# End of the attention stage ordered by hand, with expert 0's first block and half of its second product ahead of the token counts

## The chip, the cores and the metric

One NeuronCore of a Trainium2 chip runs the whole program in one launch. Its engines work side by side, each through its own list of instructions: TensorE (PE, the matrix products), VectorE (DVE), ScalarE (ACT), GpSimd (POOL) and SyncE (SP, which here only issues DMAs). The metric is the device time of one launch in microseconds; lower is better. Before the change it is 1738.94 us (median of three runs, 1738.03 to 1742.51).

## The reference

```python
# attention: q, k, v are (4, 8, 576, 64); nine chunks of 64 tokens, each by itself
scores = q_c @ k_c.T / sqrt(64); scores -= scores.max(-1)
attn = exp(scores); attn /= attn.sum(-1) + 1e-9
x = (attn @ v_c)                     # as 2304 tokens of 512
# mixture of experts, top 1, 8 experts, capacity 2304 // 8 * 2 = 576 tokens each
logits = x @ w_gate; expert = argmax(logits); gate_w = softmax(logits)[expert]
for each expert e, for its first 576 tokens in order:
    y = relu(x @ w1[e]) @ w2[e]      # 512 -> 1024 -> 512
    out[token] = gate_w * y          # the others stay zero
# second mixture, dense: P = softmax(x @ w2_gate) made doubly stochastic in 8 rounds
out = sum over e of P[:, e] * (relu(x @ w21[e]) @ w22[e])
```

The products of the experts are done with each fp32 operand split into two fp16 numbers (hi and lo), hi*hi + hi*lo + lo*hi.

## The kernel before

**Attention.** The 2304 tokens are 18 tiles of 128 (NT = 18). A loop over n runs 14 steps per iteration, each on another tile: step `f` with lag `l` works on tile n - l, in the order of the table `order`. For one tile the steps are: `st_tr` transposes K and Q on TensorE, `st_scores` the score product, `st_max` (VectorE) subtracts the row maximum and leaves `d`, `st_dtr` transposes `d`, `st_exp` (ScalarE), `st_pv` the product with V, `st_x1` (VectorE) divides and leaves the tile's `x`, `st_norm`, `st_scale`, `st_hi` and `st_lo` split `x` into fp16 rows which a DMA writes to `xs_d` in DRAM, `st_xtr`, `st_xcopy` and `st_logits` make the gate's logits. Every engine takes its instructions in the order in which this Python code issues them; nothing is reordered later.

**Routing.** Every three tiles are a group g (NG = 6). `route(g)` finds each token's expert (`r_max` to `r_tot`), its position among that expert's tokens (`r_mm` on TensorE, `r_sel`, `r_pos`), builds a table of token numbers by expert and position (`r_ge` to `r_col`, then `r_tab` on TensorE and `r_acc`, which adds it to `tacc`, for the last group to `gidx`), and the token's gate weight (`r_gw` to `r_kx`, `r_out` with its DMA to `xs_d`). The pieces are dealt out between the attention steps.

**Expert 0 early.** When group 3 (`EG`) is in the table, the first 256 tokens of expert 0 are known. `early_gather` fetches their rows into the weight area `wall`, `turn_into` transposes them into `e_xT`, and `first_product` runs four groups of 24 matmuls (L353), each followed by `hidden` (relu and split into `e_hh`, `e_hl`). This goes on beside the routing of groups 4 and 5. A matmul with `gohx` (L821) then makes the counts per expert.

**Experts.** `blocks(x, ...)` does a block of 256 or 128 tokens of expert x: first product, relu, second product (`y`, L901, 24 matmuls of 512 columns per 128 tokens), then a square sum, a scale and two writes (`x2_d`, `rk_d`). Lists called `sites` are dealt out behind its parts: the weights of the next expert are loaded (`w_load`), squared and summed (`w_stat`, L168, on ScalarE), turned into a scale (`w_scale`, L177, a small TensorE matmul that needs all four `w_stat`; `w_scale2` on VectorE), and split into hi (ScalarE) and lo (VectorE, for two quarters GpSimd) by `w_split`. Expert 0 has 512 tokens or fewer here but more than 384: after its block of 256 come two of 128 by `further`, whose rows ("late") are gathered once `gidx` is there. The raw second weights of expert 0 and expert 1 share one buffer (`stb`): expert 1's are loaded after the last split of expert 0's.

## Time and profile before

| | |
|---|---|
| median of three runs | 1738.94 us |
| the profiled execution | 1738.75 us, its span 1736.7 us |
| PE busy | 1697.3 us, 98% of the span |
| DVE, ACT, POOL busy | 69%, 54%, 42% |
| granted PE clock, mean | 0.994 |
| PE share of the chain of waits | 70% |

The profile is of one execution. Span is the time from its first to its last instruction; the execution's own time is 2.05 us longer. Busy shares are over the whole span, so a stage of 50 us hardly shows in them: the stages have to be read by windows. A granted clock of 1.00 is TensorE's 2.4 GHz, 0.50 is 1.2 GHz. In a timeline row the bracket at the end is idle time of the engine ahead of the row, with what ended it.

### The profile page before, as it was taken

How to read it: one execution, taken by the hardware profiler on the slowest of the kernel's cores; microseconds unless marked ns; L12 is line 12 of the kernel's file. 1: busy time of each engine (PE TensorE's matmuls, PEld its weight loads, DVE VectorE, ACT ScalarE, POOL GpSimd, SP SyncE). 2: the span in 40 equal slices, each digit the busy share in tenths (PEclk: the TensorE clock that was granted, in tenths of full speed). 3: DMA queues.
4: the chain of work that ended last, by engine and by line, in shares of the span. 5: the costliest groups of instructions: out<-in, count | busy, mean ns of one | idle time of the engine just before them, and what ended most of it. 6: DMA issues, size and time to landing. Idle time of an engine off the chain costs nothing.

```text
span 1736.7 us, 33835 instructions
## 1 busy us (share of the span) xinstructions
PE 1697.3 (98%) x13419; PEld 1233.8 (71%) x13419; DVE 1192.7 (69%) x2329; ACT 946.5 (54%) x1794; POOL 721.8 (42%) x765
## 2 busy tenths in 40 slices
PE   8999999989999999999999999999999999999997
PEld 7875666655555677777777777777777767777776
DVE  6886856855577766777676767677866686677554
ACT  6866756764445664655455546455643655354431
POOL 2325644622022334552445435354534543453443
PEclk9989999999999999999999999999999999999999
DMA  9948957735252413242243233223323241323201
GB/s 219 246 157 242 250 159 187 204 112 149 80 185 64 155 54 123 70 171 98 80 150 113 85 111 137 107 86 113 136 84 134 65 176 53 125 68 124 92 35 49
DMA packets 140335, 219.09 MB, mean 126 GB/s; under 512 B 62304, under 2 KB 80832, under 8 KB 140160
## 3 DMA queue, kind: packets, MB, share of 16 engines
q1 hardware_dynamic: 134768, 199.46, 36.3%
q0 software_dynamic: 5392, 17.26, 3.6%
q8 instruction: 115, 1.88, 0.5%
q14 instruction: 60, 0.49, 0.1%
HBM read 167.56 MB, written 41.91 MB: 121 GB/s over the span
## 4 chain that ended last, share of the span: by engine, by line
PE 70%; DVE 5%; ACT 1%; issue 1%; POOL 1%; POOLq 0%; ACTq 0%; DVEq 0%
PE p_m L1349 36%; PE p_m L1445 28%; PE p_m L1493 5%; DVE wall L297 3%; DVE acc L1416 1%; ACT wall L296 1%; PE p_m L1237 0%; ACT eh L1354 0%; POOL out_dram L1427 0%; DVE el L1357 0%; ACT tq L1389 0%; POOL el L1361 0%; DVE tq L1364 0%; DVE tq L1367 0%; DVE wall L255 0%
## 5 line engine op out<-in xcount | busy, mean ns | idle before, releaser
L1349 PE MATMUL p_m<-x,wall 128*128 128x384 f16 x4032 | 666.2, 326 | 3.4 <-ACT tq L1389 2.9
L1445 PE MATMUL p_m<-wall,eh 128*128 128x256 f16 x3528 | 580.3, 273 | 0.0
L1361 POOL TENSOR_TENSOR el<-tq,eh 128x384 f16<-128x384 f32 x336 | 346.9, 1060 | 560.0 <-ACT eh L1354 559.2
L1349 PEld LDWEIGHTS <-wall 128*128 128x128 f16 x4032 | 394.0, 98 | 260.3 <-issue 5.5
L1445 PE MATMUL p_m<-wall,el 128*128 128x256 f16 x1764 | 480.8, 273 | 0.0
L1354 ACT ACTIVATE eh<-tq 128x384 f16<-128x384 f32 x540 | 274.1, 522 | 189.1 <-DVE tq L1367 101.4
L1445 PEld LDWEIGHTS <-eh 128*128 128x128 f16 x3528 | 344.3, 98 | 44.3
L1416 DVE SCALAR_TENSOR_TENSOR acc<-p_m,cf,acc 128x256 f32<-128x256 f32 (+1 forms) x378 | 175.6, 521 | 130.3 <-PE p_m L1445 130.3
L1364 DVE TENSOR_TENSOR tq<-p_m,tq 128x384 f32<-128x384 f32 x288 | 158.4, 556 | 126.3 <-PE p_m L1349 125.3
L1445 PEld LDWEIGHTS <-el 128*128 128x128 f16 x1764 | 172.6, 98 | 20.0
L1357 DVE SCALAR_TENSOR_TENSOR el<-tq,eh 128x384 f16<-128x384 f32 x204 | 175.1, 860 | 10.0 <-ACT eh L1354 8.6
L1367 DVE SCALAR_TENSOR_TENSOR tq<-tq 128x384 f32<-128x384 f32 x252 | 133.1, 553 | 2.9
L353 PEld LDWEIGHTS <-wall 128*128 128x128 f16 x1344 | 108.6, 99 | 19.4 <-issue 6.1
L1389 ACT COPY tq<-p_m 128x384 f32<-128x384 f32 x96 | 45.7, 476 | 111.3 <-PE p_m L1349 107.6
L1493 PE MATMUL p_m<-wall,eh 128*128 128x512 f16 x288 | 85.6, 379 | 0.0
L1402 ACT ACTIVATE tq<-tq 128x384 f32<-128x384 f32 x84 | 43.9, 522 | 70.7 <-DVE tq L1364 70.7
L275 POOL TENSOR_TENSOR tq<-stb 128x256 f32<-128x256 f32 x56 | 48.7, 870 | 80.6 <-DVE wsumsq L184 58.9
L296 ACT ACTIVATE wall<-stb,wsb 128x256 f16<-128x256 f32 (+1 forms) x56 | 31.3, 605 | 92.0 <-DMA wb_d<-wall 66.6
L353 PE MATMUL p_p<-xT,wall 128*128 128x256 f16 x672 | 75.6, 272 | 4.8 <-PEq L1125 2.1
L275 POOL TENSOR_TENSOR tq<-sta 128x256 f32<-128x256 f32 x56 | 43.5, 776 | 82.5 <-DVE wall L297 48.7
L247 POOL TENSOR_SCALAR stb<-stb,wsb 128x1024 f32<-128x1024 f32 x16 | 54.6, 3415 | 53.6 <-DVE tq L1364 44.9
L297 DVE SCALAR_TENSOR_TENSOR wall<-stb,wsb,wall 128x256 f16<-128x256 f32 (+1 forms) x56 | 38.6, 703 | 47.1 <-ACT wall L296 44.8
(283 smaller groups left out, 2113.8 us busy)
## 6 DMA issues: line engine op xcount, KB each, us to landing
x<-xt_d SPq DMA_DIRECT2D x147, 384.0 KB, 3.6
wb_d<-wall SPq DMA_DIRECT2D x20, 896.0 KB, 3.5
wall<-wb_d SPq DMA_DIRECT2D x20, 896.0 KB, 6.4
sta<-in_moe_w_dram SPq DMA_DIRECT2D x32, 512.0 KB, 7.8
stb<-in_moe_w_dram SPq DMA_DIRECT2D x32, 512.0 KB, 6.8
sta<-in_moe_w_dram SPq DMA_DIRECT2D x16, 1024.0 KB, 6.3
stb<-in_moe_w_dram SPq DMA_DIRECT2D x16, 1024.0 KB, 7.8
xt_d<-x SPq DMA_DIRECT2D x21, 384.0 KB, 4.1
```

Of the source, the lines that this page charges most:

```text
L275: nc.gpsimd.tensor_tensor(out=at(o), in0=at(u), in1=at(v), op=op)
L297: nc.vector.scalar_tensor_tensor(out=o[:, cs, 1], in0=src, scalar=m.s, in1=o[:, cs, 0], op0=ALU.mult, op1=ALU.subtract)
L353: nc.tensor.matmul(p[:, f4, :], lhsT=w[:, kk, f * 128:(f + 1) * 128], rhs=xT[:, lo + kk, 0:W], start=(n == 0), stop=(n == 3 * KD - 1))
L1349: nc.tensor.matmul(p, lhsT=wt[:, w, lw, kk, :], rhs=xt[:, lx, kk, :], start=first and n == 0, stop=n == 5, skip_group_check=not first)
L1354: nc.scalar.activation(out=hs[op][0][:, q, :], in_=src, func=AF.Relu if op in (A11, A12, A22) or plain else AF.Copy)
L1357: nc.vector.scalar_tensor_tensor(out=hs[op][1][:, q, :], in0=src, scalar=0.0, in1=hs[op][0][:, q, :], op0=ALU.max, op1=ALU.subtract)
L1361: nc.gpsimd.tensor_tensor(out=hs[op][1][:, q, :], in0=src, in1=hs[op][0][:, q, :], op=ALU.subtract)
L1364: nc.vector.tensor_tensor(out=o, in0=a, in1=b, op=ALU.add)
L1367: nc.vector.scalar_tensor_tensor(out=o, in0=a, scalar=0.0, in1=b, op0=ALU.max, op1=op)
L1416: nc.vector.scalar_tensor_tensor(out=acc[:, j, cols], in0=y, scalar=coefs[x][:, j:j + 1], in1=acc[:, j, cols], op0=ALU.mult, op1=ALU.add)
L1445: nc.tensor.matmul(bk.t[:, cols], lhsT=hs[op][lh][:, q, t * 128:(t + 1) * 128], rhs=b.q[q][:, w, lw, :], start=m in (1, 5) and q == 0 and ...
L1493: nc.tensor.matmul(y.t, lhsT=h[:, kk % 4, c * 128:(c + 1) * 128], rhs=w[:, kk, :], start=(n == 0), stop=(n == 3 * KF - 1))
```

## The change

What it does:

- The loop over tiles ends at n = 18; what came in five more iterations is written out as one list of calls.
- K is transposed by a step of its own (`st_ktr`) at the head of an iteration; the steps `st_xtr` and `st_xcopy` move behind `st_pv`, and the routing pieces are dealt out behind `st_max` (but in iteration 18 over all steps).
- Gate weights are made in three batches (groups 0 to 2, group 3, groups 4 and 5) instead of six.
- The split of expert 0's second weights moves from iterations 20 and 21 to a place among the four groups of the first product (hi) and behind them (lo, all four). The load of expert 1's second weights (`w_load(1, "b", h)`) follows that.
- 32 of the 48 `y` matmuls of expert 0's first block (hi and lo of the hidden values by the weights' hi) come before the block itself; `blocks` then adds 8 per 128 tokens.
- The late rows are gathered into `wall` (`l_rows`) and transposed into `e_xT`, between the two halves of 128 tokens.
- The squares and sums of expert 1's second weights (the last four `next_stats`), `every[1]` (its `w_scale`) and `every[3]` (its `w_scale2`) go behind the block's second `y`.

```diff
+    l_rows = [wall[:, 4 * 4096 - 2048:4 * 4096 - 2048 + 2 * XW].bitcast(F32), wall[:, 2 * 4096 - 2 * XW:2 * 4096].bitcast(F32)]
...
-        for nm, ld, st, sc, sp in (("a", 5, 7, 10, (12, 13, 14, 15)), ("b", 12, 15, 18, (20, 20, 21, 21))):
+        for nm, ld, st, sc, sp in (("a", 5, 7, 10, (12, 13, 14, 15)), ("b", 12, 15, None, None)):
...
-        order = ((st_x1, 4), (st_scale, 5), (st_exp, 3), (st_lo, 6), (st_scores, 2), (st_hi, 5), (st_norm, 4), (st_xtr, 4),
-                 (st_max, 2), (st_xcopy, 4), (st_tr, 0), (st_pv, 3), (st_logits, 5), (st_dtr, 2))
+        order = ((st_ktr, 0), (st_x1, 4), (st_scale, 5), (st_exp, 3), (st_lo, 6), (st_scores, 2), (st_hi, 5), (st_norm, 4),
+                 (st_max, 2), (st_tr, 0), (st_pv, 3), (st_xtr, 4), (st_xcopy, 4), (st_logits, 5), (st_dtr, 2))
...
-        for n in range(NT + 6):
+        for n in range(NT + 1):
...
-            share = -(-len(queue) // len(order))
+            behind_max = [f for f, _ in order] if n == NT else [f for f, _ in order[9:]]
+            share = -(-len(queue) // len(behind_max))
...
+        st_x1(L - 2)
+        run(early_sum, early_gather)
+        for h in range(2):
+            w_load(1, "a", h)
+        st_exp(L - 1)
+        st_scale(L - 3)
+        st_xtr(L - 2)
+        st_scores(L)
...
+        st_max(L)
+        st_pv(L - 1)
+        st_lo(L - 4)
+        st_dtr(L)
...
+        st_logits(L)
+        run(*first5[:5])
+        turn_into(e_xT, e_tokens, "p")
+        run(*mm5, mid4[6])
...
+        hidden.append(next(e_first))
+        run(*tab4, *gate5, *mid5[:2], *out5, *mid5[2:])
...
+        w_split(0, "b", 0, 4, half=0)
+        hidden.append(next(e_first))
 hidden[0]()
+        run(*tab5)
+        for i in range(L - 2, NT):
+            st_lo(i)
+        run(*acc5)
+        for j in range(2):
+            nc.gpsimd.indirect_dma_start(out=l_rows[j], out_offset=None, in_=xs_d[:, :],
+                                         in_offset=bass.IndirectOffsetOnAxis(ap=gidx[:, 0, 2 + j:3 + j], axis=0))
+        w_split(0, "b", 1, 4, half=0)
...
         hidden[3]()
-        next_stats.pop(0)()
+        for h in range(4):
+            w_split(0, "b", h, 4, half=1)
+        for h in range(2):
+            w_load(1, "b", h)
+        e_y = [in_turn("p", [128, DM], F32, "p_y") for _ in range(2)]
+        for t, y in enumerate(e_y):
+            n = 0
+            for h in (e_hh, e_hl):
+                for kk in range(KF):
+                    nc.tensor.matmul(y, lhsT=h[:, kk, t * 128:(t + 1) * 128], rhs=mats[0, "b"].hi[:, kk, :], start=(n == 0), stop=False)
+                    n += 1
+        for _ in range(4):
+            next_stats.pop(0)()
...
-                    for h, w in ((hh, b.hi), (hh, b.lo), (hl, b.hi)):
+                    for h, w in ((hh, b.lo),) if begun else ((hh, b.hi), (hh, b.lo), (hl, b.hi)):
...
-                for f in [every[0], every[2], *la[:2], every[4], la[2], every[5], la[3], every[6], lb[0], every[7], lb[1]]:
+                for f in [every[0], every[2], *la[:2], every[4], la[2], every[5], la[3], *lb[:2]]:
                     f()
-                blocks(x, pre, 2, ranks(0), [[*lb[2:], *every[8:10], lambda: ahead.append(rows_ahead())], []], True,
-                       behind={(0, 4): lambda: (every[1](), every[3]()), (1, 3): late_turn, (1, 6): every[10]})
+                blocks(x, pre, 2, ranks(0), [[*lb[2:], *every[6:8], lambda: ahead.append(rows_ahead())], [*next_stats, every[1], every[3]]],
+                       True, behind={(0, KF): late_turn})
...
-                prep = [*stats, *every[11:]]
+                prep = [*every[8:], *stats]
```

How the instructions stand afterwards, at three places. First ScalarE, before the change, from the last parts of the first product to the relu of the first block of 128 (`wmxa`, `wmxb`: the four sums of squares of expert 1's first and second weights; `wall<-sta` its first weights' hi; `p_y` the block's outputs; `wall<-p_p` and `hh` relu):

```order
L358 ACTIVATE wall<-p_p 128x512 x2
L168 ACTIVATE wsq,wmxb<-stb_2089 128x1024 x2
L358 ACTIVATE wall<-p_p 128x512
L168 ACTIVATE wsq,wmxb<-stb_2089 128x1024
L358 ACTIVATE wall<-p_p 128x512
L168 ACTIVATE wsq,wmxb<-stb_2089 128x1024
L254 ACTIVATE wall<-sta_1835,wsa 128x1024 x4
L905 ACTIVATE sq_2323,ssq_2324<-p_y 128x512
```

ScalarE after the change, from the relu of the fourth group on:

```order
L360 ACTIVATE wall<-p_p 128x512
L168 ACTIVATE wsq,wmxa<-sta_1757 128x1024 x4
L254 ACTIVATE wall<-sta_1757,wsa 128x1024 x2
L342 COPY wall<-p_t 128x4x128 x2
L977 ACTIVATE sq_2295,ssq_2296<-p_y 128x512
L983 ACTIVATE row_2304<-p_y,x2s 128x2x256
L254 ACTIVATE wall<-sta_1757,wsa 128x1024 x2
L977 ACTIVATE sq_2334,ssq_2335<-p_y 128x512
L983 ACTIVATE row_2343<-p_y,x2s 128x2x256
L168 ACTIVATE wsq,wmxb<-stb_2145 128x1024 x4
```

The four squares of `wmxb` moved from between the relus to behind the scaled output row of the block's second 128 tokens.

TensorE after the change, around the small matmul that sums `wmxb` (`p_y` is the block's second product, `p_t` the late rows' transposes, `p_p` the first product of the block of 128 that follows):

```order
L882 MATMUL p_tab<-gohx,ones_170 128x16
...
L177 MATMUL p_sum<-wmxa,ones_85 128x4
...
L340 MATMUL p_t<-id_83,wall 128x128
...
L973 MATMUL p_y<-wall 128x512
L177 MATMUL p_sum<-wmxb,ones_85 128x4
L1099 TENSOR_LOAD reg_i
L355 MATMUL p_p<-wall 128x128
```

That matmul stands right ahead of the following block's first product; before, it stood among the first `y` matmuls.

VectorE after the change, at the head of iteration 18 (`x_1664` is tile 14's output, `d` the scores of tile 16):

```order
L626 TENSOR_TENSOR ohsum_101<-ohsum_102,gohs 128x8
L674 TENSOR_TENSOR tacc<-tacc,p_tab 128x144
L694 SCALAR_TENSOR_TENSOR gkx_1659<-pos_187,cap,ggw_1422 128x9
L524 TENSOR_SCALAR rs<-p_x 128x8
L525 RECIPROCAL rs<-rs 128x8
L527 TENSOR_TENSOR x_1664<-p_x,rs 128x512
```

Before the change the same place reads:

```order
L509 TENSOR_SCALAR rs<-p_x 128x8
L510 RECIPROCAL rs<-rs 128x8
L512 TENSOR_TENSOR x_1684<-p_x,rs 128x512
L677 SCALAR_TENSOR_TENSOR gkx<-gpos,cap,ggw 128x3
L659 TENSOR_TENSOR tacc<-tacc,p_tab 128x144
```

`tacc` and `gkx` have moved from behind tile 14's three rows to ahead of them.

## Rows read from the trace of the kernel before

**Rows 1.** Windows: busy us and count per engine, PEclk, DMA share, GB/s.

```profile
15.00:100.00 85.00, 84.04 (x1091) 74.29 (x1087) 69.22 (x221) 73.39 (x138) 18.94 (x26) 1.00 0.92 219
100.00:134.00 34.00, 29.19 (x244) 24.83 (x243) 27.12 (x94) 20.05 (x37) 10.55 (x12) 0.80 0.53 188
112.50:122.50 10.00, 10.00 (x58) 8.69 (x57) 7.44 (x23) 6.75 (x11) 2.73 (x3) 0.50 0.08 29
```

**Rows 2.** Timeline of PE: start, us, line, operation, [idle before <- releaser].

```profile
101.64 0.65 PE L489 MATMUL p_t<-ident,d 128*128 128x128 f32 x4 [1.50 <-DVE d L482]
...
117.91 5.12 PE L353 MATMUL p_p<-wall 128*128 128x256 f16 x24
...
123.06 2.78 PE L353 MATMUL p_p<-wall 128*128 128x256 f16 x24
...
133.50 0.17 PE L821 MATMUL p_tab<-gohx,ones 128*128 128x16 f16 x1
...
137.23 4.69 PE L901 MATMUL p_y<-wall 128*128 128x512 f16 x21
...
147.48 5.75 PE L353 MATMUL p_p<-xTc,wall 128*128 128x128 f16 x96 [0.33 <-ACT xTc L340]
```

**Rows 3.** Timeline of DVE, tile 14 and 16 in iteration 18.

```profile
95.29 0.69 DVE L512 TENSOR_TENSOR x<-p_x,rs 128x512 f32<-128x512 f32 x1
...
96.53 0.30 DVE L659 TENSOR_TENSOR tacc<-tacc,p_tab 128x144 f32<-128x144 f32 x1 [0.42 <-PE p_tab L603]
...
100.89 0.69 DVE L482 TENSOR_TENSOR d<-p_s,mx 128x512 f32<-128x512 f32 x1
```

**Rows 4.** Timeline of ACT: squares, splits, copies and output rows.

```profile
122.91 1.06 ACT L168 ACTIVATE wsq<-sta 128x1024 bf16<-128x1024 f32 x1
...
124.09 1.06 ACT L168 ACTIVATE wsq<-sta 128x1024 bf16<-128x1024 f32 x1
...
131.51 1.06 ACT L168 ACTIVATE wsq<-stb 128x1024 bf16<-128x1024 f32 x1 [4.12 <-DMA stb<-in_moe_w_dram]
...
137.10 4.26 ACT L254 ACTIVATE wall<-sta,wsa 128x1024 f16<-128x1024 f32 x4 [0.17 <-DVE wsa L90]
141.28 0.57 ACT L905 ACTIVATE sq<-p_y 128x512 bf16<-128x512 f32 x1
141.75 0.19 ACT L905 ACTIVATION_READ_ACCUMULATOR sq<-p_y 128x1 f32 x1
144.19 0.69 ACT L911 ACTIVATE row<-p_y,x2s 128x512 f16<-128x512 f32 x1 [2.25 <-DVE x2s L90]
...
146.85 1.06 ACT L340 COPY xTc<-p_t 128x512 f16<-128x512 f16 x2
```

**Rows 5.** Timeline of DVE: lo splits and copies of transposed rows.

```profile
138.28 2.49 DVE L255 SCALAR_TENSOR_TENSOR wall<-sta,wsa,wall 128x1024 f16<-128x1024 f32 x2 [1.04 <-ACT wall L254]
...
147.46 0.91 DVE L341 COPY xTc<-p_t 128x512 f16<-128x512 f16 x2 [1.65 <-ACT xTc L340]
149.00 3.16 DVE L255 SCALAR_TENSOR_TENSOR w<-stb,wsb,w 128x1024 f16<-128x1024 f32 x1 [0.62 <-ACT w L254]
...
179.58 2.48 DVE L255 SCALAR_TENSOR_TENSOR wall<-sta,wsa,wall 128x1024 f16<-128x1024 f32 x2 [0.35 <-ACT wall L254]
```

**Rows 6.** Timeline of SP: the load of expert 1's second weights.

```profile
125.85 0.94 SPq L157 DMA_DIRECT2D stb<-in_moe_w_dram  x2
```

**Rows 7.** Timeline of PE: the program's first transposes, and K's of two iterations later.

```profile
5.03 1.94 PE L461 MATMUL p_t<-ident,k 128*128 128x128 f32 x8 [5.03 <-DMA k<-in_k_dram]
6.92 3.50 PE L456 MATMUL p_t<-ident,q 128*64 128x128 f32 x32
...
19.73 1.04 PE L461 MATMUL p_t<-ident,k 128*128 128x128 f32 x8
```

**Rows 8.** Timeline of POOL: two pieces of the weight split.

```profile
148.95 2.13 POOL L248 TENSOR_TENSOR w<-stb,w 128x1024 f16<-128x1024 f32 x1
...
178.12 2.90 POOL L247 TENSOR_SCALAR stb<-stb,wsb 128x1024 f32<-128x1024 f32 x1 [2.91 <-ACT wall L246]
```

More of the change, by code (lines that the diff above doesn't have):

```diff
@@ L426 @@
         ST = [dict() for _ in range(NS)]
-        GT = [dict() for _ in range(NG)]
+        batches = (range(0, EG), range(EG, EG + 1), range(EG + 1, NG))
+        BT = {}
+        for n, gs in enumerate(batches):
+            made = dict(n=n, g0=gs[0], tiles=len(gs) * G, last=gs[-1])
+            for nm, shape, dtype in (("h", [], I32), ("inv", [], F32), ("pos", [], F32), ("ex", [E], F32)):
+                made[nm] = bd.tile([128, len(gs) * G, *shape], dtype, name=f"{nm}{n}")
+            for g in gs:
+                BT[g] = made
         def load_qk(i):
@@ L458, in st_tr @@
                     continue
-                p = in_turn("p", [128, PR, 128], F32, "p_t")
-                for pr in range(PR):
-                    nc.tensor.transpose(p[:, pr, :], src[:, 2 * pr + half, :, :].rearrange("p t d -> p (t d)"), ident)
+                p = src[half]
                 hs = slice(64 * half, 64 * half + 64)
@@ L767 @@
             for part in parts:
-                if len(part) == 1:
+                if part and part[0].__name__ in ("r_mm", "r_tab"):
                     part[0]()
@@ L778 @@
                     r()
[L779 to L781 removed]
+                if f in behind_max:
+                    for r in queue[:share]:
+                        r()
+                    queue = queue[share:]
             for f in todo.pop(n, ()):
                 f()
[L784 to L789 removed]
@@ L790 @@
-            if n >= NT + 4:
-                hidden.append(next(e_first))
-                for r in mm if n == NT + 5 else ():
-                    r()
-                w_split(0, "b", n - NT - 2, 4, half=1)
-                for _ in range(3 if n == NT + 4 else 1):
-                    next_stats.pop(0)()
-                if n == NT + 5:
-                    for h in range(2):
-                        w_load(1, "b", h)
-        for n in sorted(todo_r):
-            for part in todo_r[n]:
-                for r in part:
-                    r()
@@ L804, with run @@
-        for r in [gw, eps, rec, sel, pos, kx, rout, *second]:
-            r()
-        hidden[0]()
+        assert not (todo or todo_r or hooks)
+        first4, mm4, gate4, mid4, tab4, _, _ = route(NG - 2)
+        first5, mm5, gate5, mid5, tab5, out5, acc5 = route(NG - 1)
+        L = NT - 1
+        def run(*fs):
+            for f in fs:
+                f()
+        st_x1(L - 2)
[3 more added lines that the diff above has]
+        st_exp(L - 1)
@@ new lines @@
+        st_scale(L - 3)
+        st_xtr(L - 2)
+        st_scores(L)
+        st_hi(L - 3)
+        st_norm(L - 2)
+        st_max(L)
+        st_pv(L - 1)
+        st_lo(L - 4)
+        st_dtr(L)
+        st_xcopy(L - 2)
+        st_logits(L - 3)
+        st_exp(L)
+        st_x1(L - 1)
+        w_scale(0, "b")
+        w_alloc(0, "b")
+        st_xtr(L - 1)
+        run(*first4)
+        st_pv(L)
+        st_xcopy(L - 1, nc.scalar.copy)
+        st_scale(L - 2)
+        st_norm(L - 1)
+        st_hi(L - 2)
@@ L807 @@
+        w_split(0, "b", 1, 4, half=0)
         hidden.append(next(e_first))
-        for r in [*tab, tot1, tot2, racc]:
-            r()
         hidden[1]()
-        next_stats.pop(0)()
-        next_stats.pop(0)()
+        run(*first5[5:])
+        w_split(0, "b", 2, 4, half=0)
         hidden.append(next(e_first))
+        hidden[2]()
+        w_split(0, "b", 3, 4, half=0)
         tot = sm("gtot", [128, 2, E, E], F16)
@@ L947 @@
         pre = (None, e_tokens)
-        late = gather(tokens(0, 2, 3))
+        late = [(gidx[:, 0, 2 + j:3 + j], l_kg[:, j:j + 1], l_rows[j][:, 0:DM].bitcast(F16)) for j in range(2)]
         rows = gather(tokens(1, 0, 1))
```

133 lines of the change are left out of this document (74 added, 59 removed).

## The prediction

> **What bounds the kernel now.** I read the windows first, then TensorE's timeline from 100 us to 160, then ScalarE's, VectorE's, SyncE's and GpSimd's over the same stretch. From 15 to 100 us TensorE is busy 84.04 of 85.00 us at a granted clock of 1.00 [rows 1]: the order of the attention loop can win 1 us at most. From 100 to 134 it is busy 29.19 of 34.00 us at a mean clock of 0.80, and from 112.5 to 122.5 it works without a gap at 0.50, the lower of its two levels (1.2 GHz) [rows 1]. Two moments serve as marks below. E is the count matmul behind the first product of expert 0's first block, at 133.50; F is the start of the next block's first product, at 147.48 [rows 2]. So F is E + 13.98. What the change does to the time is what it does to E, to F - E, and to what follows F; later stages keep their order, and TensorE bounds them, so a shift at F stays to the end.
>
> **The change part by part.** The sum starts from the profiled execution's 1738.75 us, which is 0.19 below the median of 1738.94.
>
> *The loop.* The K transposes in a step of their own add no work, and the batches take small VectorE rows off an engine that is not the bound: 0, with 1 us to either side. The cover is TensorE's own queue.
>
> *Iteration 18.* Before, tile 14's `x` was made at 95.29, ahead of `tacc`, which waited until 96.53 for the position counts [rows 3]. Now `tacc` and `gkx` stand ahead of it, so the three rows of tile 14 (1.1 us) run behind 96.53, and VectorE, which from there on worked without a gap up to tile 16's `d` (100.89 and 0.69 long) [rows 3], comes there about 1.2 us later. TensorE already waited 1.50 us for that `d` [rows 2]; it now waits longer. The early gather, whose index stands behind it, is late by as much.
>
> *To the mark E.* Ends first. The four groups of 24 matmuls begin at 117.91 and E is 15.59 us later [rows 2]. A group takes 2.65 us at full clock (123.06 to the next row; 2.78 with its last matmul's own length), and the first took 5.12 at the half [rows 2]; four groups and the two table products (0.35 each) need 11.5. So 4.1 us is there to win if the first group starts where it did and the clock is up. If the clock falls again in the last tiles' many short matmuls, as it did at 112.5 [rows 1], nothing is won. The first group starts no earlier: 1.2 us are lost at `d`, and the last two tiles still go TensorE, VectorE, TensorE for `d` and `x`; what the denser list saves pays for that. The outer end would be a tail with no idle time and no half clock at all: 29.19 us busy, less half of the 10 us and of some 3 more at 0.50 around 104, is about 22.7, so E at about 122.7, 10.8 earlier. The other end is 1 us later than before. I take E 2 us earlier, between 4.1 and 0.
>
> *From E to F.* TensorE has the 32 early `y` matmuls (0.216 each by 21 in 4.53 us [rows 2], so 6.9), the sum of `wmxa`, 8 more `y`, 16 transposes, 8 more `y`: 11.5 us of work. Then comes the small matmul that sums `wmxb`, and behind it in TensorE's queue everything else. It needs four squares that now stand last in ScalarE's list, behind both of the block's output rows. ScalarE gets going on that list when `wmxa` is summed, at E + 7.1. Its own work from there: four hi splits, 4.26; two copies, 1.06; two square sums with their read-out, 0.66 each; two output rows, 0.69 each; four squares 1.18 apart, 4.72 [rows 4]. That is 12.7 us, so E + 19.8 without any wait. But it waits three times for VectorE: 0.7 for the scale of the first weights; then each output row needs a scale that stands in VectorE's queue behind two lo splits (2.49 a pair) and, the first time, the two copies of late rows (0.91) [rows 5]. With hi split 1 done at E + 8.9, the pair, the copies and the small rows end at E + 12.9, where ScalarE was free at 11.7: 1.2 of waiting. The second pair ends at 17.2, its scale at 17.5, ScalarE was free at 16.4: 1.1. So the fourth square ends at E + 22.9 and F is E + 23.0. Were ScalarE's list no obstacle, the load would be: the four lo splits of expert 0 end near E + 6.3, the load behind them lands 5.66 us later (issued at 125.85, first used at 131.51 [rows 4, 6]), the squares take 4.7: E + 16.7. Before, these squares ran between the relus, and their load was issued at 125.85 [rows 6], ahead of E. F - E thus grows by 9.0 us, with 5.9 (no waits) and 11 (late rows or a port in the way) as ends, and TensorE stands idle some 11.5 us ahead of F.
>
> *Behind F.* The work is as before, but TensorE comes from a long wait. At the program's start, after 5.03 us of idle, 8 transposes took 1.94 us that later take 1.04, and the 32 behind them took 3.50 [rows 7]: the first 5.4 us ran at the half rate, a loss of 2.7 at most. The block behind F has 5.75 us of matmuls before its first relu is due [rows 2]. I take 2.0, with 0 and 2.7 as ends. Further, two lo splits now stand on VectorE between the two relu parts of that block, while GpSimd splits its quarters. One such split took 1.24 without GpSimd (two in 2.49) and 3.16 beside GpSimd's subtraction at 148.95, but two took 2.48 beside its multiplication at 178.12 [rows 5, 8]. I take 0.3 more for each, 0.6.
>
> The Trainium skill ("SBUF — State Buffer", Who interferes with whom) says that a VectorE instruction with two SBUF inputs contends with a GpSimd one that reads SBUF, that the port pair is an exclusive lock, and that the loser blocks fully. The 3.16 fits that, the 2.48 does not. By that rule alone both splits would be held up.
>
> The sum: 1738.75 - 2.0 + 9.0 + 2.0 + 0.6 = 1748.35, say 1748.4.
>
> **The rivals.**
> 1. *The tail wins more than the wait costs (faster).* One mechanism: the written-out list keeps TensorE without a gap and at full clock from 100 us to E, so that E comes 10.8 earlier, and ScalarE's list runs without a wait, so that F - E grows by only 5.9, with no loss behind F. For it: 4.8 us of idle time and the half clock lie in that stretch [rows 1]. Against it: the 1.2 us at `d`, and the last tiles' round trips. It gives 1738.75 - 10.8 + 5.9 = 1733.9. With the 9.0 as I have it, the time turns below that of before only where E comes more than 9 us earlier. Chance 0.08.
> 2. *Both about cancel.* The clock stays up from 106 us on (E 4.1 earlier), VectorE is not in ScalarE's way (5.9 to 7), and the clock behind F is not lost: 1738.75 - 4.1 + 6.4 = 1741.1. Chance 0.14.
> 3. *VectorE is locked out.* As forecast, but both lo splits behind F take 3.16: 3.8 more instead of 0.6, 1751.6. Its rows are the 3.16 against the 2.48. Chance 0.12.
> 4. *No change in place.* That TensorE does not wait for `wmxb` would need another order than the one on its list; I give it nothing.
>
> **How the numbers follow.** The forecast, with its neighbours down to 1744, has 0.66. About 0.3% (5.2 us) is what a measurement of this kernel can tell from no change. Slower is the forecast and rival 3, 0.78; same is rival 2, 0.14; faster is rival 1, 0.08. The low end of the range takes in rival 2, 1741; the high end is E not earlier at all, 11 for F - E, 2.7 and 2.5 behind it, which is 1755. Rival 1 and a little on either side stay out.
>
> **What would show it.** Right: the `wmxb` matmul (now L177 behind L973) has about 11 us of idle time ahead of it, put down to ScalarE's squares (L168), and these begin just behind the second output row (L983); the count matmul (L882) lies near 131.5; the first rows behind F at a clock of 0.50. Tile 16's `d` ends near 102.8. Wrong: the squares done before the block's 16 last `y` matmuls, or E before 125, or a wait ahead of F under 5 us. If F lies near 154 and the end is still not later, TensorE does not bound what follows, and the step on later stages failed.

## The result, and the profile after

The changed kernel takes 1752.15 us (median of four runs, 1750.04 to 1753.59), the kernel before 1740.05 (four runs, 1738.03 to 1742.51): a ratio of 1.0068, 95% interval 1.005 to 1.0086. The profiled execution of the changed kernel took 1750.04 us, 11.3 more than that of before.

TensorE's timeline after the change, the rows that answer to [rows 2] (start, length, line, operation, idle time ahead and its releaser):

```profile
115.23 2.80 PE L355 MATMUL p_p<-wall 128*128 128x256 f16 x24
...
127.93 0.17 PE L882 MATMUL p_tab<-gohx,ones 128*128 128x16 f16 x1
...
150.40 0.59 PE L177 MATMUL p_sum<-wmxb,ones 128*128 128x4 f32 x2 [10.89 <-ACT wsq L168]
151.08 7.44 PE L355 MATMUL p_p<-wall 128*128 128x128 f16 x96
...
164.63 0.39 PE L973 MATMUL p_y<-wall,hl 128*128 128x512 f16 x1 [2.86 <-DVE hl L361]
...
168.18 5.82 PE L355 MATMUL p_p<-wall 128*128 128x128 f16 x96
...
181.36 4.28 PE L355 MATMUL p_p<-xT,wall 128*128 128x256 f16 x24 [2.18 <-PEq L1206]
```

E is at 127.93, F at 151.08. The 10.89 us ahead of the sum of `wmxb` are the wait that the prediction named, with the releaser that it named. Of the 11.3 us, E gives back 5.57 (133.50 to 127.93), F - E takes 9.17 (13.98 to 23.15), the block behind F 4.86 (17.10 from F to the third block's first product, 12.24 before), and everything behind that 2.83.

ScalarE between E and F, which answers to [rows 4]:

```profile
135.75 2.19 ACT L254 ACTIVATE wall<-sta,wsa 128x1024 f16<-128x1024 f32 x2 [2.45 <-DVE wsa L90]
...
140.56 0.69 ACT L983 ACTIVATE row<-p_y,x2s 128x512 f16<-128x512 f32 x1 [1.08 <-DVE x2s L90]
...
145.09 0.69 ACT L983 ACTIVATE row<-p_y,x2s 128x512 f16<-128x512 f32 x1 [1.19 <-DVE x2s L90]
145.67 1.05 ACT L168 ACTIVATE wsq<-stb 128x1024 bf16<-128x1024 f32 x1
...
149.20 1.06 ACT L168 ACTIVATE wsq<-stb 128x1024 bf16<-128x1024 f32 x1
```

The four squares begin at the end of the second output row, without a wait. From the scale of the first weights on (135.75), the waits in the list ahead of them are the two for a row's scale, 1.08 and 1.19 (1.2 and 1.1 were forecast).

Behind F, VectorE and GpSimd (these answer to [rows 5, 8]):

```profile
142.32 2.48 DVE L255 SCALAR_TENSOR_TENSOR wall<-sta,wsa,wall 128x1024 f16<-128x1024 f32 x2
...
159.62 4.35 DVE L255 SCALAR_TENSOR_TENSOR w<-stb,wsb,w 128x1024 f16<-128x1024 f32 x2 [2.42 <-ACT w L254]
163.89 0.68 DVE L361 SCALAR_TENSOR_TENSOR hl<-p_p,hh 128x512 f16<-128x512 f32 x1
```

The second of the two splits at 159.62, shown by itself:

```profile
160.82 3.15 DVE L255 SCALAR_TENSOR_TENSOR w<-stb,wsb,w 128x1024 f16<-128x1024 f32 x1
```

```profile
157.61 2.86 POOL L247 TENSOR_SCALAR stb<-stb,wsb 128x1024 f32<-128x1024 f32 x1 [18.10 <-ACT w L246]
160.55 2.34 POOL L248 TENSOR_TENSOR w<-stb,w 128x1024 f16<-128x1024 f32 x1
```

Two lo splits take 2.48 with GpSimd idle and 4.35 beside its work, and they stand ahead of the second half of `hl`, for which TensorE waits 2.86. The two are not hit alike: the first, which starts beside GpSimd's multiplication (L247), takes 1.28 us as it would alone, and all of the excess lies in the second, which starts 0.27 us behind GpSimd's subtraction (L248).

The windows (busy us and count of PE, PEld, DVE, ACT, POOL, then granted clock, DMA share, GB/s; they answer to [rows 1]):

```profile
97.00:128.00 31.00, 25.45 (x271) 22.56 (x272) 24.48 (x97) 17.56 (x32) 11.89 (x13) 1.00 0.41 140
...
145.00:156.00 11.00, 5.51 (x56) 5.42 (x57) 1.68 (x9) 5.29 (x10) 0.00 (x0) 0.54 1.04 384
...
165.00:169.00 4.00, 4.00 (x20) 1.92 (x18) 4.00 (x4) 1.27 (x4) 3.92 (x3) 0.57 0.01 2
```

In this execution the clock stays at 1.00 up to E (before: 0.80 in the mean from 100 to 134). It is down twice behind E: 0.54 in the stretch with the 10.89 us of waiting, 0.57 behind the 2.86.

### The profile page after: what moved, and what is told of

It reads as the page before. It is cut to its first block, busy times and chain, and to the rows that moved or that the text cites. A ratio compares the mean times of both kernels' runs of the same rounds, so it can differ in the third digit from the quotient of the medians.

```text
span 1748.3 us, 33814 instructions
## 1 busy us (share of the span) xinstructions
PE 1693.5 (97%) x13419; PEld 1233.4 (71%) x13419; DVE 1190.8 (68%) x2311; ACT 946.3 (54%) x1795; POOL 719.0 (41%) x760
## 4 chain that ended last, share of the span: by engine, by line
PE 69%; DVE 5%; ACT 1%; issue 1%; POOL 1%; POOLq 0%; ACTq 0%; DVEq 0%
PE p_m L1427 36%; PE p_m L1523 28%; PE p_m L1571 5%; DVE wall L297 3%; DVE acc L1494 1%; ACT wall L296 1%; PE p_m L1315 0%; ACT eh L1432 0%; POOL out_dram L1505 0%; DVE el L1435 0%; ACT tq L1467 0%; DVE tq L1442 0%; POOL el L1439 0%; DVE tq L1445 0%; DVE wall L255 0%
## 5 line engine op out<-in xcount | busy, mean ns | idle before, releaser
L247 POOL TENSOR_SCALAR stb<-stb,wsb 128x1024 f32<-128x1024 f32 x16 | 53.7, 3354 | 78.4 <-DVE tq L1442 45.9
```

## The experiments

All kernels but the one with iteration 18 changed (g1) are the same program as the changed kernel up to E. E, F and the start of expert 1's first product are read from each kernel's one profile; the ratio is to the kernel before, run beside it. In the diffs small functions are written by what they do (`skip`, `count`, `rows_ahead`, `whole`), without their `lambda`, and lines that only follow from those shown are left out.

| kernel | median us | ratio [95%] | E | F - E | expert 1 - E |
|---|---|---|---|---|---|
| before | 1740.05 | | 133.50 | 13.98 | 37.66 |
| changed | 1752.15 | 1.0068 [1.005, 1.0086] | 127.93 | 23.15 | 53.43 |
| e1_scale_later | 1741.95 | 1.0013 [1.0, 1.0026] | 130.28 | 11.41 | 48.73 |
| e2_squares_first | 1748.32 | 1.0045 [1.0028, 1.0062] | 130.88 | 21.22 | 48.46 |
| e3_splits_later | 1747.43 | 1.0042 [1.0027, 1.0056] | 131.55 | 23.38 | 53.03 |
| e4_keep_busy | 1750.28 | 1.0057 [1.0039, 1.0075] | 131.10 | 23.49 | 48.28 |
| g1_behind_max | 1751.41 | 1.0057 [1.0036, 1.0078] | 130.40 | 24.28 | 55.35 |
| f1_order | 1745.35 | 1.0038 [1.0024, 1.0052] | 130.50 | 11.42 | 50.47 |
| f3_all_later | 1745.41 | 1.0031 [1.0018, 1.0043] | 128.51 | 11.43 | 51.17 |
| f4_splits_last | 1751.55 | 1.0061 [1.0047, 1.0074] | 131.26 | 11.42 | 46.80 |
| f5_both_splits_last | 1750.85 | 1.0055 [1.0041, 1.007] | 129.26 | 11.42 | 44.88 |
| f7_inside | 1737.99 | 0.9992 [0.998, 1.0004] | 128.93 | 11.42 | 38.83 |
| f8_turn_early | 1738.75 | 0.9989 [0.9976, 1.0002] | 129.59 | 11.41 | 35.07 |

### The sum and the scale moved behind F

```diff
-[*next_stats, every[1], every[3]]
+[*next_stats]
...
-further(2, [[skip, count, *prep[0:4]],
+further(2, [[skip, count, every[1], every[3], *prep[0:4]],
```

> The changed kernel, with only the sum of expert 1's second weights (the small matmul and its scale, every[1] and every[3]) moved one step on: from ahead of the first product of the block of 128 to between that product's two halves. E is the count matmul, F the start of that first product; the changed kernel has F at E + 23.15 after 10.89 us of idle time. Theory (ScalarE's list): the squares still end near E + 22.3, but TensorE now starts F near E + 12.2, as soon as the late rows are copied, and waits between the halves instead, until E + 23; the second product of that block, which began at E + 30.4, begins near E + 26. Time 4 to 5.5 us under the changed kernel's, 1745 to 1748. Rival (something else behind the second output row holds TensorE, such as the late rows or the read of the counts): F stays near E + 23 and the time within 1 us of the changed kernel's.

TensorE:

```profile
141.69 3.15 PE L355 MATMUL p_p<-wall 128*128 128x128 f16 x48
152.75 0.59 PE L177 MATMUL p_sum<-wmxb,ones 128*128 128x4 f32 x2 [7.91 <-ACT wsq L168]
...
162.69 0.39 PE L973 MATMUL p_y<-wall,hl 128*128 128x512 f16 x1 [2.01 <-DVE hl L361]
```

F comes at E + 11.4, as soon as TensorE's own work allows; the matmul then waits in its new place, behind 48 matmuls, 7.91 instead of 10.89. The sum comes at the same distance from E as in the changed kernel (22.5), so ScalarE's list, and nothing on TensorE, sets that time. The median falls by 10.2 us, about twice the 4 to 5.5 expected, and is 1.3 above that of the kernel before beside it, which the interval hardly tells from nothing. Where the other half comes from is not shown: between the two profiled executions (8.1 us) 2.4 lie ahead of expert 1's start, 1.5 in its first group, which runs at full clock here (2.78 against 4.28), and 4.3 further on, in stages whose program is the same.

### The squares ahead of the second output row

```diff
-[[*lb[2:], *every[6:8], rows_ahead], [*next_stats, every[1], every[3]]]
+[[*lb[2:], *next_stats, *every[6:8], rows_ahead], [every[1], every[3]]]
```

> The changed kernel, with the four squares of expert 1's second weights behind the block's first output row instead of its second; their sum stays where it is. Theory (ScalarE's list): the first output row ends near E + 13.3, the four squares take 4.7 from there, so F is near E + 18.5 instead of E + 23.15, the idle time ahead of it 6.2 instead of 10.9 us, and the time 3.5 to 5 us under the changed kernel's. Rival (the load that now stands behind the four lo splits is the bound): it was issued at E + 6.4 and its median landing is 8.3 us, so that the third square can't start before E + 15 and, if the later loads of expert 2 share the transfer engines, not before E + 18; then F stays at E + 21 or later and 2 us at most are won.

ScalarE, and the load on SyncE's queue:

```profile
149.20 1.06 ACT L168 ACTIVATE wsq<-stb 128x1024 bf16<-128x1024 f32 x1 [2.79 <-DMA stb<-in_moe_w_dram]
```

```profile
137.24 1.00 SPq L157 DMA_DIRECT2D stb<-in_moe_w_dram  x2
```

F moves by only 2 us, as the rival had it: now the third square waits for the load, whose second half lands 12 us after its issue (5.66 before the change [rows 4, 6]). With the load landing there, two squares and the sum still follow, so no order of ScalarE's list brings the sum before about E + 20.7; the prediction's bound by the load, E + 16.7, was 4 us short. The median is 3.8 lower all the same. Expert 1 starts 5.0 nearer to E, and only 1.9 of that is F: 1.9 more is a shorter wait at the branch ahead of expert 1 (0.30 against 2.18). Four loads of expert 2's weights are issued 2.4 us behind it; that they are what slows it was not tried.

### The splits behind the second relu

```diff
-[[skip, count, *prep[0:4]], [*prep[4:], next_count],
+[[skip, count], [*prep, next_count],
```

> The changed kernel, with the four pieces of the split of expert 1's second weights behind both relu parts of the block of 128 instead of between them. In the changed kernel the second product of that block takes 9.83 us, 2.86 of them waiting for VectorE's second relu part, which stands behind two lo splits (4.35 us beside GpSimd). Theory: that wait goes, the second product takes 5.5 to 6.3 us, and the time falls by 3 to 4.5 us, since expert 1 needs these splits only some 25 us later. Rival: the splits are then late for expert 1's second product and a wait there takes the gain back: time within 1 us of the changed kernel's, with TensorE waiting for the hi or lo split in expert 1.

```profile
154.93 6.91 PE L355 MATMUL p_p<-wall 128*128 128x128 f16 x96 [0.32 <-issue]
166.85 5.52 PE L355 MATMUL p_p<-wall 128*128 128x128 f16 x96
176.00 1.04 PE L973 MATMUL p_y<-wall,hh 128*128 128x512 f16 x2 [3.62 <-ACT hh L360]
```

The block behind F takes 11.9 us (17.1 in the changed kernel) and no longer waits for `hl`: the two splits were that wait. But the third block's relu now stands behind the same splits and squares on ScalarE, and TensorE waits 3.62 for it. The wait moved one block down: the third block, with the branch behind it, takes 4.6 us more (17.73 against 13.18), so expert 1 starts only 0.4 nearer to E, where the block behind F had won 5.2. The median is 4.7 lower all the same (1747.43); the profiled execution, at 1752.60 the slowest of ten, doesn't show where.

### TensorE kept at work ahead of F

46 matmuls of 512 columns stand ahead of the sum, and nothing uses their result.

```diff
+def busy():
+    p = in_turn("p", [128, DM], F32, "p_d")
+    for _ in range(46):
+        nc.tensor.matmul(p, lhsT=id16, rhs=mats[0, "b"].hi[:, 0, :], start=True, stop=True)
...
+[*next_stats, busy, every[1], every[3]]
```

> The changed kernel, with 46 matmuls of 512 columns (9.9 us) added on TensorE ahead of the sum of expert 1's second weights; they write a bank that nothing reads, and fill the 10.9 us in which TensorE waits for ScalarE. Nothing else moves. Theory (the clock after the wait): F stays at E + 23.2, but the granted clock behind it is 1.00 instead of 0.50, the 96 matmuls of the first product take 5.6 to 5.8 instead of 7.44 us, and the time falls by 1.7 to 3.5 us. Rival (the matmuls behind F are slow for another reason, such as the transfers that ran at full share there): 7.4 us as before, and no change in time.

```profile
153.57 0.39 PE L177 MATMUL p_sum<-wmxb,ones 128*128 128x4 f32 x2 [0.96 <-ACT wsq L168]
...
154.59 5.52 PE L355 MATMUL p_p<-wall 128*128 128x128 f16 x96 [0.63 <-issue]
...
166.21 0.39 PE L973 MATMUL p_y<-wall,hl 128*128 128x512 f16 x1 [2.86 <-DVE hl L361]
...
168.38 5.52 PE L355 MATMUL p_p<-wall 128*128 128x128 f16 x96
```

F stays at E + 23.5, but the 96 matmuls behind it take 5.52 instead of 7.44: the half clock costs 1.9 us there, and it goes when the wait is filled. The wait for `hl` (2.86) is the same, so it isn't the clock's; but here the clock stays at 1.00 behind it, and the whole block from F to the third takes 13.79 instead of 17.10, 3.3 less. Expert 1 starts 5.2 nearer to E, with 1.9 of it at the branch (0.30 of waiting instead of 2.18). Little of this reaches the end: the median is 1.9 lower, with overlapping runs (1749.15 to 1752.09 against 1750.04 to 1753.59), and the profiled execution is no faster.

### Iteration 18

```diff
-behind_max = [f for f, _ in order] if n == NT else [f for f, _ in order[9:]]
+behind_max = [f for f, _ in (order[8:14] if n == NT else order[9:])]
```

> The changed kernel with one edit: in the last iteration of the attention loop (iteration 18) the routing rows stand on VectorE behind the maximum and the difference d of tile 16, and no longer from the iteration's start on. The prediction's step was that these rows make d of tile 16 late, 1.2 us of waiting on TensorE in the way of E. If the step holds and nothing takes its place: d of tile 16 ends 1 to 3 us earlier (101.55 in the changed kernel's profile), the transposes of d start near 99.5 instead of 101.7, E comes 1 to 2 us earlier and the time is 1 to 2 us less, 1749 to 1751. Rival: the table product of the early gather, next in TensorE's queue, needs the same routing rows and waits in the place of d: the transposes move, but the idle time only changes its releaser (cols instead of d), E stays within 0.6 us, and the time is the changed kernel's, 1751 to 1753.

```profile
98.74 0.63 PE L504 MATMUL p_t<-ident,d 128*128 128x128 f32 x4
102.09 0.28 PE L669 MATMUL p_tab<-cols,rows 128*128 128x144 f16 x1 [2.72 <-POOL cols L663]
102.93 0.40 PE L669 MATMUL p_tab<-cols,rows 128*128 128x144 f16 x2 [0.56 <-POOL cols L663]
```

`d` is transposed 3 us earlier (101.69 in the changed kernel), and the table product behind it waits 3.28 us for its columns instead. The time stays (1751.41), and E, at 130.40, lies among the others. The rival holds for this move: the 1.2 us at `d` only change their place, since the next matmul needs the rows that made `d` late.

### All of it between and behind the relus of the next block

`f1_order` puts the four squares between the two relus of the block of 128, and sum, scale, splits and expert 2's squares behind its output row; `f3_all_later` puts two squares behind each relu, expert 2's behind the second, and the rest behind the row.

```diff
-[*next_stats, every[1], every[3]]]
+[]]
...
+f1: further(2, [[skip, count, *next_stats], [next_count], [every[1], every[3], *prep, *later]])
+f3: further(2, [[skip, count, *next_stats[:2]], [*next_stats[2:], *stats, next_count], [every[1], every[3], *every[8:], *later]])
```

> The changed kernel, with all that stood at the second site of expert 0's first block (expert 1's four squares of the second weights, the sums and the scale) taken behind it: the squares stand between the two relus of the next block, and the sum, the scale, the splits and expert 2's squares behind that block's output row. Marks as in the prediction: E the count matmul, F the first product of the next block. Theory A (the wait ahead of F is ScalarE's list, and the time won there is kept): F = E + 11.5 to 12 and no wait for L168 ahead of it; the second relu of the block then stands behind four squares and the load, so its second product starts near E + 21.5 and the third block's relus behind the splits and squares (near E + 36); expert 1 begins near E + 42 (E + 53.4 in the changed kernel's profile, E + 48.7 with only the scale moved), and the time is 6 to 10 us under the changed kernel's, 1736 to 1743. Theory L (the load is what ends last, wherever the squares stand): the sum ends no earlier than with the squares moved first, E + 21, but nothing on TensorE waits there: F as under A. Theory B (the time is set behind this stretch: expert 1 waits for its second weights, split later now): F as under A, expert 1 early, but its second product starts no earlier than before, and the time is that of the scale moved alone, 1742.

> As the kernel with the squares between the relus, but two squares of expert 1's second weights stand behind each relu of the block of 128, expert 2's squares behind the second, and only the sum, the scale and the four splits behind its output row: so the third block's relus stand behind some 4.4 us of ScalarE's splits and not 9.1. Theory A: F = E + 11.5 to 12, the block's second product near E + 18.5 to 21 (the second relu waits at most for the load), the third block's first product near E + 25 to 27, its second near E + 32 to 34, expert 1 near E + 37 to 40; the time 1731 to 1738, under that of the kernel before. Theory B (expert 1 waits for its second weights): expert 1 early by as much, but then a wait on TensorE for these splits of 3 us and more, and a time of 1740 or above.

TensorE in `f1_order`, then ScalarE in `f3_all_later`:

```profile
158.08 0.28 PE L177 MATMUL p_sum<-wmxb,ones 128*128 128x4 f32 x2
...
170.85 1.03 PE L973 MATMUL p_y<-wall,hh 128*128 128x512 f16 x2 [7.11 <-ACT hh L360]
...
174.23 0.61 PE L973 MATMUL p_y<-wall,hl 128*128 128x512 f16 x1 [2.35 <-DVE hl L361]
```

```profile
162.42 0.69 ACT L983 ACTIVATE row<-p_y,x2s 128x512 f16<-128x512 f32 x1 [4.08 <-DVE x2s L90]
164.51 2.19 ACT L246 ACTIVATE w<-stb,wsb 128x1024 f16<-128x1024 f32 x2 [1.40 <-DVE wsb L90]
166.60 2.17 ACT L254 ACTIVATE w<-stb,wsb 128x1024 f16<-128x1024 f32 x2
168.68 1.06 ACT L360 ACTIVATE hh<-p_p 128x512 f16<-128x512 f32 x2
```

The sum now waits for nothing, and F is at E + 11.4 in both. But the third block's relus stand behind the 9 us that were moved, and TensorE waits 7.11 and 2.35, in the other kernel 8.15 and 2.43, then works at the half clock. Both are 3.4 us above the kernel with the scale alone moved: theory A had F right and the times too low (1736 to 1743, 1731 to 1738). In `f1_order` the third block's relus come at E + 40 where I had E + 36; in `f3_all_later` I had left out VectorE's four reductions, which make the output row 4.08 late and with it the splits. They are late themselves because expert 2's second weights are: VectorE waits 2.88, 2.35 and 0.45 for that load, of which this is the first:

```profile
154.43 1.22 DVE L170 TENSOR_REDUCE wmxb<-stb 128x1 f32<-128x1024 f32 x1 [2.88 <-DMA stb<-in_moe_w_dram]
```

### The splits behind the third block

```diff
-    [*next_stats[2:], *stats, next_count], [every[1], every[3], *every[8:], *later]])
+    [*next_stats[2:], *stats[0::2], next_count], [every[1], every[3], *stats[1::2], *later]])
...
 with tc.If(rc > 384): further(3)
+for f in every[8:]: f()
 with tc.If(more[0] > 512): whole()
```

`f5_both_splits_last` besides takes `every[6:8]` from the first block to behind the second relu of the next.

> The kernel with all moved later (two squares behind each relu of the block of 128, the scale behind its output row), with two things moved once more: expert 1's four splits of the second weights behind the third block, and VectorE's four reductions of expert 2's second weights behind the scale. In the kernel that it starts from, the relus of the third block stood behind a row that waited 4.08 us for these reductions and 4.3 us of splits: TensorE waited 8.15 for the relu, 2.43 for VectorE, and the second product then took 10.4 us instead of 5.2, at the half clock. Theory A (what each list of ScalarE and VectorE makes late is all that holds TensorE in this stretch): F = E + 11.5, the second block's product near E + 20, the third block's first product near E + 26, its second near E + 33 with under 1.5 us of waiting for the relu, expert 1 at E + 38 to 41 (E + 51 in the kernel that it starts from), and, as the splits then lie beside expert 1's first product (8 us and more of work), no wait for them of more than 1 us; the time 1733 to 1738, under the kernel before by 0.15 to 0.4%. Theory B (the work of the other engines is the bound, not its place): expert 1's second product or the sum behind its first group waits for splits, scale or reductions by what was won, 6 us and more, and the time is 1741 to 1746.

> As the kernel with the splits behind the third block, and besides two splits of expert 1's first weights (4.7 us on ScalarE and VectorE with their wait) taken from the first block to behind the second relu of the block of 128. Theory A: the first relu of that block comes near E + 15 instead of E + 17.5, the second output row of the first block too; the block's second product begins near E + 18.5, and all behind it is 1 to 2 us earlier than with the splits left there: expert 1 at E + 36.5 to 39.5, the time 1731 to 1737. Theory B: expert 1's first product waits for these splits, or expert 2's squares come late for its sum, and the time is that of the other kernel or 1 to 3 us more.

TensorE in `f5_both_splits_last`, and VectorE ahead of the branch:

```profile
166.26 0.61 PE L973 MATMUL p_y<-wall,hl 128*128 128x512 f16 x1 [5.20 <-DVE hl L361]
...
182.71 0.56 PE L177 MATMUL p_sum<-wmxa,ones 128*128 128x4 f32 x2 [5.79 <-DVEq L1208]
```

```profile
161.02 4.59 DVE L170 TENSOR_REDUCE wmxb<-stb 128x1 f32<-128x1024 f32 x4
165.53 1.28 DVE L361 SCALAR_TENSOR_TENSOR hl<-p_p,hh 128x512 f16<-128x512 f32 x2
...
178.16 4.34 DVE L255 SCALAR_TENSOR_TENSOR w<-stb,wsb,w 128x1024 f16<-128x1024 f32 x2 [2.23 <-ACT w L254]
```

Expert 1 starts 4 to 6 us earlier, and the time is 5 to 6 us longer. Two places hold TensorE in `f5_both_splits_last`: the reductions stand ahead of `hl` (5.20), and the branch stands behind the splits. VectorE is through the branch at L1208 when its splits end, at 182.5, and the sum in expert 1's first product starts at 182.71. Theory B had a wait at that sum, though not the branch as its cause, and less of it in the time (1741 to 1746). Between expert 1 and expert 2 this kernel takes 30.8 us, `f1_order` 22.7; it loses some 5.5 us more behind expert 2: 2.2 between the sums of experts 2 and 3, where TensorE waits for relus and `hl`, and part in half-clock stretches (0.94 from 320 to 340, 0.91 from 380 to 400, 1.00 in `f1_order`); I did not follow it further.

### Inside the branch, and the transposing DMAs earlier

```diff
-[*next_stats[2:], *every[6:8], *stats[0::2], next_count], [every[1], every[3], *stats[1::2], *later]
+[*next_stats[2:], *every[6:8], next_count], [every[1], every[3], *later]
...
 with tc.If(rc > 384) as third:
-    further(3)
+    further(3, [[], prep, []])
+with third.Else():
+    for f in prep: f()
...
-prep = every[8:]
+prep = [*every[10:], *every[8:10], *stats[1::2], *stats[0::2]]
```

The last line changes an order too: VectorE's two splits now come ahead of the two that GpSimd does, on ScalarE's list and on VectorE's.

`f8_turn_early` issues `turn_dma(rows)` at the first block's first site, ahead of the second row's store.

> The kernel with both splits moved, with expert 1's four splits of the second weights and expert 2's squares and reductions put inside the branch of the third block, behind its second relu (and into that branch's other arm for fewer tokens), where ScalarE and VectorE had nothing to do for 13 and 8 us. In the two kernels with the splits behind the branch, VectorE reached the next branch only behind them, and TensorE then waited 2.30 and 5.79 us for VectorE's queue in expert 1's first product; the four reductions ahead of the third block's lo parts held its second product 4.78 and 5.20 us, and the half clock came on top. Theory A (what each list makes late is all that holds TensorE in this stretch): no wait of over 1.5 us between F and expert 1 but the two for relus (under 1 each); F = E + 11.5, the third block's first product near E + 23, its second near E + 29, expert 1 at E + 35 to 39 (E + 40.5 before relative to the E of the changed kernels is 171.16 - 130.5), VectorE's list behind it up to 3 us late for the sum in expert 1's first product, and the time 1732 to 1738, 0.1 to 0.5% under the kernel before. Theory B (the work of the other engines is the bound, not its place): the waits reappear as before, 5 us and more, at the sum behind expert 1's first group or at its second product, and the time is 1741 or above.

> The kernel with the splits inside the third block's branch, with one more step moved: the two transposing DMAs that turn expert 1's first rows stand on SyncE's queue ahead of the store of the first block's second output row and no longer behind it. In the kernel that it starts from, this store waited on the queue until 159.16 (its row was written at 146), the transposes were issued at 160.67, and expert 1 waited 5.16 us for them and then ran 5.30 instead of 2.78 in its first group, at the half clock. Theory A: the transposes are issued near 150.5, expert 1 starts near E + 34 (E + 38.8 before) with under 1 us of waiting and at full clock, and the time is 5 to 7 us less, 1731 to 1733.5, 0.35 to 0.5% under the kernel before. Theory D (the transposes are slow because the queues are full of loads, not because they are issued late): they end when they did, near 167, or the loads behind them are late by as much, and the time stays at 1737 to 1739.

TensorE in `f7_inside`, then VectorE:

```profile
151.74 0.28 PE L177 MATMUL p_sum<-wmxb,ones 128*128 128x4 f32 x2
151.88 5.52 PE L355 MATMUL p_p<-wall 128*128 128x128 f16 x96
...
167.76 5.30 PE L355 MATMUL p_p<-xT,wall 128*128 128x256 f16 x24 [5.16 <-DMA xT<-xg]
```

```profile
159.10 2.48 DVE L255 SCALAR_TENSOR_TENSOR w<-stb,wsb,w 128x1024 f16<-128x1024 f32 x2 [0.34 <-ACT w L254]
161.50 4.59 DVE L170 TENSOR_REDUCE wmxb<-stb 128x1 f32<-128x1024 f32 x4
```

From E to the end of the third block the timeline shows no wait on TensorE, and VectorE's two splits, both begun before GpSimd's first piece (161.25), take 2.48. Whether the place or the new order of the splits did that, this run can't tell. The time is 1737.99: 14.2 us under the changed kernel, and not told apart from the kernel before. This is the best evidence that the loss came from the order of the other engines' work. What is left is the wait for expert 1's rows. Moving their DMAs takes that away:

```profile
164.66 2.78 PE L355 MATMUL p_p<-xT,wall 128*128 128x256 f16 x24 [1.56 <-PEq L1210]
170.06 0.36 PE L177 MATMUL p_sum<-wmxa,ones 128*128 128x4 f32 x2 [2.62 <-DVEq L1210]
...
191.32 2.78 PE L355 MATMUL p_p<-xT,wall 128*128 128x256 f16 x24 [1.55 <-DMA xT<-xg]
```

Expert 1 is 3.8 us nearer to E and at full clock, but 2.62 go to VectorE at the branch and 1.55 to the next expert's DMAs, and the time stays: theory D's time, by other waits than the one it named. That from here on the other engines and the queues hold the stretch as tightly as TensorE does is my reading of these waits; no run took them away.

## Why the prediction was right

The sign came out, and so did the wait that was named, at the place and length forecast. That the time came so near (1748.4 forecast, 1750.04 in the profiled execution, 1752.15 in the median) is partly luck: in the profile E came 3.6 us earlier than forecast, the block behind F cost 2.3 more and the later stages 2.8 more, and these misses nearly cancel.

- *Loop, 0 ± 1.* The scores of tile 16 start at 95.42, 1.0 earlier than before: at the edge of the bound. In e3, with the same program, they start at 96.50, so not all executions have this.
- *Iteration 18.* `tacc` is ahead of tile 14's `x` and `d` ends at 101.55, 1.25 earlier than the 102.8 forecast, since the loop ahead was faster; from the scores on it is 1.0 later than before. The order did it, but taking it away gives nothing (g1).
- *E, -2.0.* The profiled execution has -5.57, beyond the -4.1 that I took as the likely end. I had the first of the four groups start no earlier; it starts at 115.23, 2.7 earlier than before, and E follows 12.70 behind it (15.59 before), mostly because the clock never fell. In the ten experiments with the same program up to E it lies between 128.51 and 131.55, and the median of all eleven is 130.28: -3.2, of which 1.4 is the earlier start of the first group (116.50 in the median). So the size came near for most executions, and the start was wrong in all. For the kernel before there is one profile, at the half clock (5.12 in its first group); how its E varies is not known.
- *F - E, +9.0.* Measured +9.17; the sum of `wmxb` waits 10.89 (11.5 forecast), for ScalarE's squares. e1 shows it by moving the matmul, e2 shows the load close behind as the next bound, later than I had it.
- *Behind F, +2.6.* Measured +4.86. The first product takes 1.7 more (7.44 against 5.75; 2.0 forecast), at the half clock; but before, TensorE then waited 0.77 for the relu, and now it doesn't, so the second product starts only 0.75 later behind F. The other 4.1 are in the second product (9.83 against 5.72): the wait of 2.86 for `hl`, and the half clock behind it. e4 takes both losses of the clock away and leaves the wait. My 2.0 came from rows that don't show the clock: the matmuls at the program's start took twice their later time, but the granted clock there is 1.00 (5.00 to 10.40). The splits are the step that failed: I had 0.6 for them and no wait. They stand on VectorE ahead of the second `hl`, and wait 2.42 there for ScalarE's part; their own excess of 1.87 comes on top. Without that excess the wait would be about 1.0 (an estimate: 2.86 less 1.87). e3 takes the splits away and the wait goes.
- *The splits' length.* I read the 3.16 and the 2.48 as two prices and took a value near the lower. The traces show one rule with two outcomes, by which engine starts first. At 149.00 the split starts 0.05 behind the subtraction and takes 3.16. At 179.58 the second split (180.78) is under way when the subtraction starts, and it is GpSimd that is held, 2.95 instead of 2.13:

```profile
181.10 2.95 POOL L248 TENSOR_TENSOR wall<-stb,wall 128x1024 f16<-128x1024 f32 x1
```

  In the changed kernel the second split again starts behind the subtraction (160.82 against 160.55) and ends 1.08 us after it. In the thirteen traces 88 splits of this size start while such a subtraction runs, and each ends 1.08 or 1.09 us after it. The Trainium skill ("SBUF — State Buffer", Who interferes with whom) has the port pair as an exclusive lock; these rows agree, for the subtraction. They do not for all of the multiplication: the first split starts 2.0 us into one and takes 1.28, as alone. So not both splits are held up, as I had it by that rule (3.8, rival 3), but the one that starts second.
- *Later stages, 0.* +2.83, and not by TensorE's order of matmuls: expert 1's first group runs at the half clock (4.28 against 2.78) behind a wait at the branch of 2.18 (0.74 before). TensorE's own branch instruction takes 5.26 us there (3.85 before, 0.38 in e4, where the wait is 0.30); what sets its length no run shows. That the end follows F by a constant failed: the profiled execution's time less the start of expert 1 is 1567.6 us before and 1568.7 after the change, 1562.9 in e1, 1574.9 in f4 and 1577.8 in f5.

With E at its median over the eleven executions, -3.2, the terms give 1738.75 - 3.2 + 9.2 + 4.9 + 2.8 = 1752.45, near the median of the changed kernel, 1752.15. It is a check of the terms' size and no more: they come from one profile each, and the later stages vary by more than the difference.

## What to carry to other kernels

When a small instruction that sums something moves in TensorE's list, work out the list of the engine that feeds it from the last point both share; its length is the wait, and here it came out 0.6 us too long (11.5 against 10.89). Moving the feeding work out of the way only helps if the place it goes to has room: five kernels here (e3, f1, f3, f4, f5) moved some or all of the same ScalarE and VectorE work to the next relu or the next branch, and lost much of what they had won, until in f7 it stood behind the third block's second relu, inside the branch. Work that one engine has ahead of a branch can hold another behind it: in f4, f5 and f8 TensorE waited 2.30, 5.79 and 2.62 for VectorE to get through. And where VectorE and GpSimd both split, look which of the two starts first.

## What the runs showed of the hardware

- The same program shows the half clock in its tail in some kernels' executions and not in others: the first group of 24 took 2.80 us in the changed kernel, f3, f5 and f7, 3.19 in f8, and 4.14 to 4.45 in e1 to e4, f1 and f4. E lies up to 3.6 us apart, of which 1.1 is there already at tile 16's scores (96.50 in e3, 95.42 in the changed kernel).
- The clock need not fall behind a wait: behind the same 2.86 us it was 0.57 in the changed kernel and 1.00 in e4, where TensorE had been kept at work before.
- A VectorE split of 128x1024 (two inputs from SBUF, the on-chip memory) takes 1.28 us alone. Started while GpSimd's subtraction of the same size runs, it ends 1.08 or 1.09 after that (88 of 88 cases); under way when the subtraction starts, it takes 1.28 and the subtraction is longer (2.3 to 3.2 instead of 2.1 alone, 126 of 126 cases). GpSimd's multiplication by a scalar held only splits that started 2.1 us or more before its end; those that started 1.8 or less before it took 1.27 to 1.29.
- TensorE's branch instruction ahead of expert 1 took from 0.38 (e4) to 6.74 us (f4). Only its last part shows as a wait, up to 2.84 (f4).
- The queues: a load issued ahead of six others took 12 us to its second half's landing (e2). The two transposing DMAs held SyncE's queue for 8.75 us when issued at 151.68 (f8), and 2.71 at 160.67 (f7); that the loads then in flight were the cause was not tried:

```profile
151.68 8.75 SPq L929 DMA_TRANSPOSE xT<-xg  x2
```
